# A delta-rule recurrence with a squared-ReLU feed-forward: the hand-written order of a program is replaced by a graph and a list builder

## The chip, the cores and the metric

The kernel runs on one NeuronCore of a Trainium2 chip. Its engines are TensorE (PE, with weight loads shown apart as PEld), VectorE (DVE), ScalarE (ACT), GpSimd (POOL) and SyncE (SP); each works through its own instructions in the order in which the program issues them. The metric is the time of one execution in microseconds (us) on the device.

## The reference

There are B=4 batches, H=8 heads, S=768 steps of time and D=40 columns. For each batch and head a 40 x 40 state is carried through time, and the outputs of all heads, put side by side (320 columns), go through a feed-forward layer of 2048 hidden columns:

```
state = 0
for t in range(768):
    y[t]  = r[t] @ state
    Sa    = state @ a[t]
    state = state * w[t] - outer(Sa, b[t]) + outer(v[t], k[t])
x = y with heads side by side                 # 3072 x 320
out = (max(x @ w_in, 0) ** 2) @ w_out         # 320 -> 2048 -> 320
```

## The kernel before

**Tiles and steps.** Time is cut into 6 chunks of 128 steps of time. Within a chunk the recurrence becomes matrix products between the 128 steps. A "batch" m (24 of them) is one chunk of one of the four batches of the data, with all 8 heads. A "step" st (48) is half of that, four heads, held as two pairs of heads. Eight steps make a chunk, and the state of a chunk goes to the next through the tile UZ.

**Preparing a batch.** Six loads (L81, queue of SP) bring w, k, b, a, v, r as NW to NR, with four buffers each; a small memset on POOL (L80) holds a later batch's loads back. prep_ln, prep_decay: logarithm of w, its running sum by a product (cs, L197), two exponentials GI and GA on ScalarE. POOL multiplies k and b by GI (KB, L206) and casts a, v, r (L183); prep_v copies v again from RV into EVX (L190). prep_kb, prep_ga, prep_rv turn these tiles on TensorE (tt, L214) and bring them out of PSUM as KBT, GT, AT and RVT.

**A step.** st_a_mm and st_a_ev: products ca (L260), masked into CN (VectorE, L268). st_p: products P. st_m: P is copied as Mc (ScalarE). st_corr, st_c1, st_corr, st_sn: two corrections of P by CN, with c1 on VectorE (L306) between them; ScalarE writes the result, negated, as Sn into EVX (L314). st_t: Sn and the carried state UZ are turned (tb, L339 and L345) and copied as TB (L350). st_ex_mm, st_ex_ev: products ex (L364), masked into EVX (L370). st_z, st_kb: products uy (L379, L389). st_y: uy becomes YS, the output of the step (L399), and UZ (L404).

**Half-array products.** ca and ex contract over 64 rows, and two of them stand in the upper and the lower half of the array; tb and uy write 64 columns each and stand side by side. The others use the whole array.

**Feed-forward.** It goes by "halves" h (12): four steps make one. gather copies a few rows within YS by four DMAs (L436) so that 8 heads of 40 rows lie in three groups. ffn_in makes a block of hidden columns (hp, L451; ReLU hs on ScalarE, L459; square Gt on POOL or VectorE, L461), eight a half. ffn_out sums over them (op, L478), two row blocks of two parts, copied out and stored (L482, L484).

**The order** is written by hand. The main loop runs over st and issues st_a_mm(st + 1), st_ex_mm(st - 1), st_p(st), st_y(st - 2) and so on; prepare(st, lot) issues a batch's preparation by a table, and filler(st) takes one hp or half an op from a queue that feed fills two steps after the gather. PSUM banks have fixed uses: two for ff (hp, op, cs, KB turned), ca0, ca1, ex0, ex1, sp (P, tb) and uy. warm(n) issues products without use, 54 in all.

Of the kernel before, what the change touches and what calls it, by code (L numbers as in the profile page):

```python
# [9 lines left out]
I32 = mybir.dt.int32  # L10
# [8 lines left out]
def kernel(  # L19
# [12 lines left out]

# [14 lines left out]
    AHEAD = 4  # L55
    HB = NB // 2
    NEV = 6

    gl = ctx.enter_context(tc.tile_pool(name="gl", bufs=1))
    chp = ctx.enter_context(tc.tile_pool(name="chp", bufs=2))  # L60
    qdp = ctx.enter_context(tc.tile_pool(name="qdp", bufs=3))
    ffp = ctx.enter_context(tc.tile_pool(name="ffp", bufs=3))
    ps = ctx.enter_context(tc.tile_pool(name="ps", bufs=1, space=PSUM))
    nat_cm = tc.tile_pool(name="natp", bufs=AHEAD)
# [7 lines left out]
    nat_srcs = {"W": w, "K": k, "V": v, "R": r, "A": a, "B": b}  # L72
    nat = {}

    def load(m, gate=True):
        c, bb = divmod(m, NB)
        for key in ("W", "K", "B", "A", "V", "R"):
            t_ = natp.tile([128, NHH, D], FP32, name=f"N{key}", tag=f"N{key}")
            if gate and key == "W":
                nc.gpsimd.memset(t_[0:1, 0, 0:1], 0.0)  # L80
            nc.sync.dma_start(  # L81
                out=t_[:],
                in_=nat_srcs[key][bb, :, c * L:(c + 1) * L, :].rearrange("h t e -> t h e"))
            nat[key, m] = t_

    for m in range(AHEAD):
        load(m, gate=False)
# [7 lines left out]
    ones_f = gl.tile([128, 128], FP32, name="ones_f")  # L95
    nc.gpsimd.memset(ones_f[:], 1.0)
    UTI = gl.tile([128, 128], FP32, name="UTI")
# [4 lines left out]
    ones_b = gl.tile([128, 128], BF16, name="ones_b")  # L102
    nc.vector.memset(ones_b[:], 1.0)
    nc.vector.memset(ACC[:], 0.0)
    IDb = gl.tile([128, 128], BF16, name="IDb")
# [4 lines left out]


    def warm(n):
        wu = ps.tile([128, 128], FP32, name="wu", tag="uy")
        for i in range(n):
            nc.tensor.matmul(out=wu[:], lhsT=ones_b[:], rhs=ones_b[:], start=True, stop=True)

    warm(26)
    MEX = gl.tile([128, 4, L], BF16, name="MEX")
# [6 lines left out]
    pads = {}  # L125
    for key, n in (("KB", 4), ("GA", 2), ("RV", 2)):
        pads[key] = []
        for i in range(n):
            t_ = gl.tile([128, len(key), NHH, 64], BF16, name=f"{key}p{i}")
            nc.vector.memset(t_[:, :, :, D:64], 0.0)  # L130
            pads[key].append(t_)
    MCN = gl.tile([128, 2, 2, L], BF16, name="MCN")
# [3 lines left out]
    GTs, RVs, EVXs, UZs, WIN = [], [], [], [], []  # L136
    for i in range(4):
        GTs.append(gl.tile([128, PB, L + 2], BF16, name=f"GT{i}"))
        nc.gpsimd.memset(GTs[i][:, :, 0:1], 1.0)
    for i in range(NEV):  # L140
        EVXs.append(gl.tile([128, 2, 2, EV], BF16, name=f"EVX{i}"))
        nc.gpsimd.memset(EVXs[i][:, :, :, 2 * LV:EV], 0.0)
    for i in range(4):
        t_ = gl.tile([128, 2, PB, LV], BF16, name=f"RV{i}")
        nc.gpsimd.memset(t_[:, :, :, L:LV], 0.0)
        for s in range(2):
            o_ = 64 * s
            nc.gpsimd.tensor_copy(  # L148
                out=t_[o_:o_ + D, 0, :, L:LV],
                in_=IDb[o_:o_ + D, o_:o_ + D].rearrange("p (u d) -> p u d", u=1)  # L150
                .to_broadcast([D, PB, D]))
        RVs.append(t_)
    for i in range(2):
        UZs.append(gl.tile([128, NP, 128], BF16, name=f"UZ{i}"))
    for g in range(PB - 1):
        WIN.append(gl.tile([128, DFF], BF16, name=f"WIN{g}"))
    for t_ in (UZs[1], WIN[2]):
        nc.vector.memset(t_[:], 0.0)
# [6 lines left out]
    bt = {}  # L165
# [4 lines left out]
    def prep_ln(m):  # L170
        o = bt[m] = Batch()
        o.RV, o.GA = (pads[key][m % 2] for key in ("RV", "GA"))
        o.KB = pads["KB"][m % 4]
        o.GT, o.RVT = GTs[m % 4], RVs[m % 4]
        o.EVX = [EVXs[(2 * m + u) % NEV] for u in range(2)]
        o.lnW = ffp.tile([128, NHH * D], FP32, name="lnW", tag="lnW", bufs=2)
        nc.scalar.activation(out=o.lnW[:], in_=nat.pop(("W", m))[:].rearrange("p h e -> p (h e)"),
                             func=ACTF.Ln)

    def prep_cast(m):  # L180
        o = bt[m]
        for key, pad in (("A", o.GA[:, 1]), ("V", o.RV[:, 1]), ("R", o.RV[:, 0])):
            nc.gpsimd.tensor_copy(out=pad[:, :, 0:D], in_=nat.pop((key, m))[:])  # L183
            if key == "V" and m == 0:
                prep_v(m)

    def prep_v(m):
        o = bt[m]
        for u in range(2):
            nc.gpsimd.tensor_copy(  # L190
                out=o.EVX[u][:, :, :, L:LV].rearrange("p i s e -> p (i s) e"),
                in_=o.RV[:, 1, 4 * u:4 * u + 4, 0:D])

    def prep_decay(m):
        o = bt[m]
        cs = ps.tile([128, NHH, D], FP32, name="cs", tag="ff", bufs=2)
        nc.tensor.matmul(out=cs[:].rearrange("p h e -> p (h e)"), lhsT=UTI[:], rhs=o.lnW[:],  # L197
                         start=True, stop=True)
        GI = ffp.tile([128, NHH, D], FP32, name="GI", tag="GI", bufs=2)
        nc.scalar.activation(out=GI[:], in_=cs[:], func=ACTF.Exp, scale=-1.0,  # L200
                             accum_out=ACC[:, AI + m:AI + m + 1])
        nc.scalar.activation(out=o.GA[:, 0, :, 0:D], in_=cs[:], func=ACTF.Exp,
                             accum_out=ACC[:, AG + m:AG + m + 1])
        for u, key in enumerate("KB"):
            eng = nc.vector if m < 2 and key == "B" else nc.gpsimd
            eng.tensor_tensor(out=o.KB[:, u, :, 0:D], in0=nat.pop((key, m))[:], in1=GI[:],  # L206
                              op=ALU.mult)

    def turned(pad, us=(0, 1), t_=None, **home):
        if t_ is None:  # L210
            t_ = ps.tile([128, 2, PB, L], BF16, name="tt", **home)
        for u in us:
            for j in range(PB):
                nc.tensor.transpose(  # L214
                    out=t_[:, u, j, :], identity=IDb[:],
                    in_=pad[:, u, 2 * j:2 * j + 2, :].rearrange("p a b -> p (a b)"))
        return t_

    def prep_rv(m):
        o = bt[m]  # L220
        t1 = turned(o.RV, tag="ex0")
        nc.vector.tensor_copy(out=o.RVT[:, :, :, 0:L], in_=t1[:])

    def prep_kb(m):
        o = bt[m]
        o.KBT = chp.tile([128, 2, PB, L], BF16, name="KBT", tag="KBT", bufs=3)
        t2 = turned(o.KB, tag="ff", bufs=2)
        nc.scalar.activation(out=o.KBT[:], in_=t2[:], func=ACTF.Copy)  # L228

    def prep_ga(m):  # L230
        o = bt[m]
        if m > 0:
            prep_v(m)
        o.AT = chp.tile([128, PB, L], BF16, name="AT", tag="AT", bufs=3)
        if m == 0:
            t3 = turned(o.GA, us=(0,), tag="ex0")
            nc.scalar.activation(out=o.GT[:, :, 1:L + 1], in_=t3[:, 0], func=ACTF.Copy)
            prep_kb(m)
            turned(o.GA, us=(1,), t_=t3)
        else:  # L240
            t3 = turned(o.GA, tag="ex0")
            nc.scalar.activation(out=o.GT[:, :, 1:L + 1], in_=t3[:, 0], func=ACTF.Copy)  # L242
        nc.vector.tensor_tensor(out=o.AT[:], in0=t3[:, 1], in1=o.GT[:, :, 0:L], op=ALU.mult)  # L243
# [3 lines left out]
    def where(st):  # L247
        c, q = divmod(st, NQ)
        return c, bt[c * NB + q // 2], (q % 2) * 2, slice(2 * q, 2 * q + 2), EVXs[st % NEV]

    CNs, Ps, SnTs, TBs, uys, Mc, Cc, YSs = {}, {}, {}, {}, {}, {}, {}, {}

    def st_a_mm(st):
        c, o, j0, p2, EVX = where(st)
        ca = CNs[st, "ps"] = [ps.tile([128, 2, 2, L], FP32, name=f"ca{s}", tag=f"ca{s}")
                              for s in range(2)]
        for u in range(2):
            for i in range(2):
                for s in range(2):
                    nc.tensor.matmul(out=ca[s][:, i, u, :], lhsT=o.KBT[half(s), u, j0 + i, :],  # L260
                                     rhs=o.AT[half(s), j0 + i, :], start=(i == 0 and u == 0),
                                     stop=True, skip_group_check=True)

    def st_a_ev(st):
        ca = CNs.pop((st, "ps"))
        CN = CNs[st] = qdp.tile([128, 2, 2, 2, L], BF16, name="CN", tag="CN")
        for s in range(2):
            nc.vector.tensor_tensor(out=CN[:, :, s], in0=ca[s][:], in1=MCN[:], op=ALU.mult)  # L268
# [54 lines left out]
    def st_energy(su):  # L323
        if su < 0 or su % (NQ // 2) > 1:
            return
# [398 lines left out]
```

## Time and profile before

| what | value |
|---|---|
| runs before | 323.8, 324.98, 325.31 us; median 324.98 |
| profiled execution, first to last instruction | 321.4 us; the record gives no time of its own around this span |
| granted TensorE clock, mean | 0.945 |
| busy: PE, PEld | 280.2 us (87%), 213.1 us (66%) |
| busy: DVE, POOL, ACT | 230.8 us (72%), 207.7 us (65%), 199.7 us (62%) |
| DMA | 31.37 MB, mean 98 GB/s |

The median of the runs is 3.6 us above the profiled span. Busy times are shares of the whole span; stages differ, so the times by stage say more. Products overlap on TensorE, so intervals between starts are read there, not durations.

### The profile page before, as it was taken

How to read it: one execution, taken by the hardware profiler on the slowest of the kernel's cores; microseconds unless marked ns; L12 is line 12 of the kernel's file. 1: busy time of each engine (PE TensorE's matmuls, PEld its weight loads, DVE VectorE, ACT ScalarE, POOL GpSimd, SP SyncE). 2: the span in 40 equal slices, each digit the busy share in tenths (PEclk: the TensorE clock that was granted, in tenths of full speed). 3: DMA queues.
4: the chain of work that ended last, by engine and by line, in shares of the span. 5: the costliest groups of instructions: out<-in, count | busy, mean ns of one | idle time of the engine just before them, and what ended most of it. 6: DMA issues, size and time to landing. Idle time of an engine off the chain costs nothing.

```text
span 321.4 us, 9886 instructions
## 1 busy us (share of the span) xinstructions
PE 280.2 (87%) x3880; PEld 213.1 (66%) x3880; DVE 230.8 (72%) x519; ACT 199.7 (62%) x529; POOL 207.7 (65%) x390
## 2 busy tenths in 40 slices
PE   6766758889999999999999999999999999979892
PEld 5544445576767767777776777777777677657581
DVE  6546777688887877888888788788888768663140
ACT  4344365378577676876866776695786767625461
POOL 8368467298678669667767866866876696534400
PEclk9778597599999999999999999999999999979999
DMA  7999999964475376457537636644762000000101
GB/s 130 174 167 174 185 160 170 161 107 87 85 143 98 78 126 111 89 99 125 105 71 144 111 70 115 118 94 87 133 111 52 26 6 22 27 3 21 34 35 51
DMA packets 158455, 31.37 MB, mean 98 GB/s; under 512 B 152944, under 2 KB 158080, under 8 KB 158400
## 3 DMA queue, kind: packets, MB, share of 16 engines
q1 hardware_dynamic: 155760, 28.02, 48.5%
q0 software_dynamic: 2640, 2.63, 5.2%
q8 instruction: 32, 0.52, 0.7%
q14 instruction: 23, 0.19, 0.2%
HBM read 28.84 MB, written 3.93 MB: 102 GB/s over the span
## 4 chain that ended last, share of the span: by engine, by line
PE 71%; ACT 13%; issue 7%; DVE 5%; POOL 2%; ACTq 0%; DVEq 0%; POOLq 0%
PE hp L451 16%; PE cs L197 6%; PE tt L214 5%; PE uy L389 5%; PE ca L260 5%; PE tb L339 4%; ACT hs L459 4%; PE ex L364 3%; ACT KBT L228 3%; PE P L298 3%; ACT EVX L314 2%; PE P L276 2%; ACT GT L242 2%; PE uy L379 2%; PE tb L345 1%
## 5 line engine op out<-in xcount | busy, mean ns | idle before, releaser
L451 PE MATMUL hp<-YS,WIN 120*128 120x256 bf16 (+1 forms) x576 | 78.0, 273 | 0.1
L461 POOL TENSOR_TENSOR Gt<-hs 128x512 bf16<-128x512 bf16 x66 | 67.8, 1042 | 13.5 <-ACT hs L459 12.5
L370 DVE TENSOR_TENSOR EVX<-ex,MEX 128x512 bf16<-128x512 f32 x96 | 65.8, 686 | 4.7 <-PE ex L364 3.0
L459 ACT ACTIVATE hs<-hp 128x512 bf16<-128x512 f32 x96 | 57.6, 600 | 16.1 <-PE hp L451 14.4
L268 DVE TENSOR_TENSOR CN<-ca,MCN 128x512 bf16<-128x512 f32 x96 | 61.4, 681 | 0.8 <-PE ca L260 0.8
L451 PEld LDWEIGHTS <-WIN 120*128 120x128 bf16 (+1 forms) x576 | 49.8, 97 | 6.5 <-issue 0.5
L206 POOL TENSOR_TENSOR KBp<-NK,GI 128x320 bf16<-128x320 f32 x24 | 21.1, 880 | 38.5 <-ACT GI L200 37.1
L478 PEld LDWEIGHTS <-Gt 128*128 128x128 bf16 x384 | 35.0, 98 | 12.8 <-issue 0.2
L318 POOL TENSOR_TENSOR Cc<-x,EVX 128x160 bf16<-128x160 f32 x48 | 23.4, 487 | 25.9 <-ACT EVX L314 23.7
L317 POOL TENSOR_TENSOR x<-Mc,c 128x160 f32<-128x160 bf16 x48 | 23.3, 485 | 15.3 <-DVE c L306 14.3
L306 DVE TENSOR_TENSOR c<-P,Mc 128x160 bf16<-128x160 f32 x48 | 15.6, 325 | 23.6 <-POOL RVp L183 10.7
L320 ACT ACTIVATE jk<-CN 128x512 bf16<-128x512 bf16 x48 | 30.6, 637 | 0.0
L339 PE MATMUL tb<-IDb,EVX 128*64 128x128 bf16 x192 | 15.0, 238 | 15.7 <-ACT EVX L314 15.7
L298 PEld LDWEIGHTS <-CN 128*128 128x128 bf16 x384 | 21.0, 97 | 10.4 <-issue 9.8
L350 DVE COPY TB<-tb 128x512 bf16<-128x512 bf16 (+1 forms) x48 | 19.1, 397 | 11.2 <-PE tb L345 8.3
L228 ACT ACTIVATE KBT<-tt 128x1024 bf16<-128x1024 bf16 x24 | 24.5, 1019 | 4.1 <-PE tt L214 4.1
L291 ACT ACTIVATE Mc<-P 128x160 bf16<-128x160 f32 x48 | 14.8, 307 | 18.2 <-PE P L282 18.2
L399 DVE TENSOR_TENSOR YS<-uy,GT 128x256 bf16<-128x256 f32 x48 | 20.1, 418 | 7.0 <-PE uy L389 6.7
L339 PEld LDWEIGHTS <-EVX 128*64 128x64 bf16 x192 | 6.9, 110 | 26.9 <-ACT EVX L314 26.5
L243 DVE TENSOR_TENSOR AT<-tt,GT 128x512 bf16<-128x512 bf16 x24 | 10.2, 425 | 19.5 <-ACT GT L242 16.5
L389 PE MATMUL uy<-EVX,KBp 128*64 128x168 bf16 x384 | 23.8, 249 | 0.0
L197 PE MATMUL cs<-lnW,UTI 128*128 128x320 f32 x48 | 22.0, 544 | 0.3 <-POOL RV L148 0.3
(132 smaller groups left out, 609.9 us busy)
## 6 DMA issues: line engine op xcount, KB each, us to landing
NW<-in_w_dram SPq DMA_DIRECT2D x24, 160.0 KB, 2.8
NK<-in_k_dram SPq DMA_DIRECT2D x24, 160.0 KB, 3.7
NB<-in_b_dram SPq DMA_DIRECT2D x24, 160.0 KB, 3.6
NA<-in_a_dram SPq DMA_DIRECT2D x24, 160.0 KB, 3.9
NV<-in_v_dram SPq DMA_DIRECT2D x24, 160.0 KB, 4.6
NR<-in_r_dram SPq DMA_DIRECT2D x24, 160.0 KB, 3.6
out_dram<-osb SPq DMA_DIRECT2D x24, 160.0 KB, 1.8
WOUT<-in_moe_w_out_dram POOLq DMA_DIRECT2D x1, 1280.0 KB, 11.2
```

The source lines that it names most:

```text
L197: nc.tensor.matmul(out=cs[:].rearrange("p h e -> p (h e)"), lhsT=UTI[:], rhs=o.lnW[:], start=True, stop=True)
L228: nc.scalar.activation(out=o.KBT[:], in_=t2[:], func=ACTF.Copy)
L268: nc.vector.tensor_tensor(out=CN[:, :, s], in0=ca[s][:], in1=MCN[:], op=ALU.mult)
L298: nc.tensor.matmul(out=P[:, i, s, 0:D], lhsT=CN[:, i, s, 1, :], rhs=X[:, 2 * i + s], start=False, stop=last, skip_group_check=True)
L320: nc.scalar.activation(out=jk[:], in_=CN[:, :, :, 1, :], func=ACTF.Square, accum_out=ACC[:, AN + st:AN + st + 1])
L339: nc.tensor.transpose(out=tb[half(s), i, :], in_=EVX[:, i, s, L + LV:EV], identity=IDb[:])
L370: nc.vector.tensor_tensor(out=EVX[:, :, s, 0:2 * LV].rearrange("p i (u x) -> p i u x", u=2)[:, :, :, 0:L], in0=exs[st][s][:], in1=MEX[:].r ...
L389: nc.tensor.matmul(out=uy[half(s), i, :], lhsT=o.KB[:, u, 2 * (j0 + i) + s, :], rhs=EVX[:, i, s, LV * u:LV * u + LV], start=(c == 0 and i ...
L451: nc.tensor.matmul(out=hp[:, u, :].rearrange("p (a b) -> p a b", a=HB), lhsT=WIN[g][0:ROWS[g], j * 128:(j + 1) * 128], rhs=by_pair(c, hf)[ ...
L459: nc.scalar.activation(out=hs[:], in_=flat, func=ACTF.Relu)
L461: later.append(lambda: eng.tensor_tensor(out=out_, in0=hs[:], in1=hs[:], op=ALU.mult))
L478: nc.tensor.matmul(out=op_[:], lhsT=Gts[c, hf][:, j, b_, :], rhs=WOUT[:, j, :], start=(j == 0), stop=(j == NJ - 1))
```

## The change

The program is the same computation. Each operation now is an entry of a graph: name, engine, rank, cost, latency, what it needs, which buffers it uses. A function listed() goes through them with a clock of its own and puts them into one order; then they are issued in that order. Buffers belong to rings with a number of places each (RING); the eight PSUM banks are common to all uses, with at most four for hp and op and three for a batch's preparation. From step 12 on ca(st) and ex(st - 3) are one entry R, and uy's products of step st - 4 and tb of step st - 2 are one entry C. The V cast goes from NV into EVX directly. EVX, KB and GT have five buffers by batch. The first batch is prepared in two halves. The warm-up products after the first 26 are gone, and so are POOL's small memsets ahead of the loads.

```diff
-    def prep_v(m):
-        o = bt[m]
-        for u in range(2):
-            nc.gpsimd.tensor_copy(
-                out=o.EVX[u][:, :, :, L:LV].rearrange("p i s e -> p (i s) e"),
-                in_=o.RV[:, 1, 4 * u:4 * u + 4, 0:D])
+            if key == "X":
+                nc.gpsimd.tensor_copy(
+                    out=o.EVX.tile[:, j0:j0 + n, :, L:LV].rearrange("p i s e -> p (i s) e"),
+                    in_=o.nat["V"].tile[:, h])
...
+    NBANK = 8
+    CAP = {"ff": 4, "prep": 3}
+    RING = {"N": 4, "lnW": 2, "GI": 2, "KB": 5, "GA": 2, "RV": 2, "EVX": 5, "RVT": 4, "KBT": 3,
+            "AT": 3, "GT": 5, "CN": 3, "c1": 3, "x1": 3, "jk": 1, "jm": 1, "Mc": 2, "Cc": 2,
+            "TB": 9, "UZ": 2, "YS": 3, "hs": 3, "Gt": 2, "osb": 3}
...
+        op(("L", m, key), "DQ", rank, 0.97, 3.0, [], [o.nat[key]], go)
...
+        def go():
+            nc.gpsimd.dma_start(out=WOUT[:], in_=moe_w_out.rearrange("(j p) f -> p j f", p=128))
+        op(("WOUTq",), "DQ", -1.5, 8.3, 8.3, [], [], lambda: None)
+        op(("WOUT",), "POOL", -1.5, 0.5, 1.0, [("WOUTq",)], [], go)
...
+            def gather(p=p, row=row, hh=hh, e0=e0, n=n):
+                src = 64 * (hh % 2) + e0
+                nc.sync.dma_start(out=by_pair()[row:row + n, p], in_=by_pair()[src:src + n, hh // 2])
+            op(("mv", h, x), "SP", st0 + 7.3 + 0.01 * x, 0.1, 2.0, done, [X_], gather)
...
+            rank = st0 + 8.0 + 0.45 * jj
+            op(("hp", h, jj), "PE", rank, *pe(0.654),
+               [("mv", h, x) for x in range(len(MOVED))] + [("WIN", g) for g in range(NG)],
+               [X_, hpb], ff_in, "F")
...
+    for st in range(MERGE, NS):
+        merge(("R", st), [("ca", st), ("ex", st - 3)], st, "R")
+        merge(("C", st), [("kbm", st - 4), ("tb", st - 2)], st + 0.01, "C")
...
+    SWITCH, SLACK = 0.095, 0.06
+    BIAS = {"FR": 0.3, "FC": 0.6, "CR": 0.3}
+    START = {"PE": 4.0, "ACT": 2.2, "DVE": 4.0, "POOL": 5.2, "SP": 0.9, "DQ": 0.9}
...
+                t0 = min(t for t, _ in cand) + SLACK
+                t, o = min(((t, o) for t, o in cand if t <= t0),
+                           key=lambda x: (x[1].rank + BIAS.get(mode + (x[1].mode or mode), 0.0),
+                                          x[1].order))
...
+    plan = listed()
...
+    for t, o in plan:
...
+        o.fn()
```

In the new names kbm is the product into uy by KB, z the carried one, mv a copy of the gather, hs and Gt the ReLU and the square, and DQ a queue that exists in the list alone: the loads are issued by SP, in the list's order among SP's own entries.

More of the change, by code (lines that the diff above doesn't have):

```diff
@@ new lines, with buf, op @@
+    class Op:
+        __slots__ = ("name", "eng", "rank", "cost", "lat", "needs", "bufs", "mode", "fn", "end",
+                     "order")
+    ops, rings = {}, {}
+    def buf(ring, kind=None):
+        b_ = Buf(ring, kind)
+        if ring != "bank":
+            row = rings.setdefault(ring, [])
+            b_.n = len(row)
+            row.append(b_)
+        return b_
+    def op(name, eng, rank, cost, lat, needs, bufs, fn, mode=None):
+        o = Op()
+        o.name, o.eng, o.rank, o.cost, o.lat, o.mode = name, eng, rank, cost, lat, mode
+        o.needs, o.bufs, o.fn, o.end, o.order = list(needs), list(bufs), fn, None, len(ops)
+        for b_ in o.bufs:
+            b_.users.append(o)
+        assert name not in ops, name
+        ops[name] = o
@@ new lines, in merge @@
+    def merge(name, parts, rank, mode):
+        olds = [ops.pop(p) for p in parts]
+        bufs = []
+        for o in olds:
+            for b_ in o.bufs:
+                b_.users.remove(o)
+                if b_ not in bufs:
+                    bufs.append(b_)
+        def go():
+            for o in olds:
+                o.fn()
+        cost = sum(o.cost for o in olds)
+        op(name, "PE", rank, *pe(cost), [n for o in olds for n in o.needs], bufs, go, mode)
+        for p in parts:
+            alias[p] = name
@@ L109 @@
     )
[L112 to L118, printed above, removed]
+    for i in range(26):
+        nc.tensor.matmul(out=banks[NBANK - 1][:, 0:128], lhsT=ones_b[:], rhs=ones_b[:], start=True,
+                         stop=True)
     nc.vector.memset(MEX[:], 1.0)
@@ L153 @@
-    for i in range(2):
[L154 to L158, printed above, removed]
+    for i in range(2):
+        for ring in ("GT", "EVX", "RVT"):
+            blank(ring, i)
+    later = {}
+    for ring, a_, b_, eng, cost in (("KB", 2, 5, "DVE", 0.21), ("UZ", 1, 2, "DVE", 1.0),
+                                    ("GT", 2, 5, "POOL", 0.05), ("EVX", 2, 5, "POOL", 0.2),
+                                    ("RVT", 2, 4, "POOL", 1.1), ("UZ", 0, 1, "DVE", 1.0)):
+        for i in range(a_, b_):
+            rank = i - 1.5 if ring != "UZ" else (7.0, 0.5)[i]
+            later[ring, i] = ("blank", ring, i)
+            op(("blank", ring, i), eng, rank, cost, cost + 0.05, [], [],
+               lambda ring=ring, i=i: blank(ring, i))
@@ L160, in half, with cleared @@
+    def cleared(ring, i):
+        i %= RING[ring]
+        return [later[ring, i]] if (ring, i) in later else []
     def half(s):
         return slice(64 * s, 64 * s + 64)
-    bt = {}
+    nat_srcs = {"W": w, "K": k, "V": v, "R": r, "A": a, "B": b}
+    SPLIT = 1
     class Batch:
         pass
[L170 to L178, printed above, removed]
@@ L209, in turned @@
[L209 to L222, printed above, removed]
@@ L224, in prep_kb @@
[L224 to L243, printed above, removed]
@@ L247, in where @@
-    def where(st):
-        c, q = divmod(st, NQ)
[L249 to L257, printed above, removed]
+    bt = []
+    for m in range(NBC):
+        o = Batch()
+        bt.append(o)
+        o.nat = {key: buf(f"N{key}") for key in "WKBAVR"}
+        o.lnW, o.GI, o.KB, o.GA, o.RV, o.EVX, o.RVT, o.KBT, o.AT, o.GT = (
+            buf(x) for x in ("lnW", "GI", "KB", "GA", "RV", "EVX", "RVT", "KBT", "AT", "GT"))
+        for x in ("KB", "GA", "RV", "EVX", "RVT", "GT"):
+            getattr(o, x).tile = fixed[x][m % RING[x]]
+        o.parts = [(0, 2), (2, 2)] if m < SPLIT else [(0, PB)]
@@ new lines, in tb_ev, with ex_mm @@
+        def tb_ev():
+            hi = 4 if carry else 2
+            nc.vector.tensor_copy(out=sb(TB_, [128, 4, 128], BF16)[:, 0:hi], in_=tbv()[:, 0:hi])
+        def ex_mm():
+            R, V = o.RVT.tile[:, 0], o.RVT.tile[:, 1]
+            for u in range(2):
+                for i in range(2):
+                    for s in range(2):
+                        lhsT = TB_.tile[half(s), i, :] if u else V[half(s), j0 + i, 0:L]
+                        nc.tensor.matmul(out=quads(ex[s])[:, i, u, :], lhsT=lhsT,
+                                         rhs=R[half(s), j0 + i, 0:L], start=(i == 0 and u == 0),
+                                         stop=True, skip_group_check=True)
@@ new lines, in add_step @@
+        op(("ex", st), "PE", st + 3.0, *pe(0.225), [("TB", st), ("RVT", m, p)],
+           [TB_, o.RVT] + ex, ex_mm, "R")
+        for s in range(2):
+            op(("EVX", st, s), "DVE", st + 3.05 + 0.02 * s, 0.6, 0.685, [("ex", st)],
+               [ex[s], o.EVX], lambda s=s: ex_ev(s))
+        op(("kbm", st), "PE", st + 4.01, *pe(0.285),
+           [("EVX", st, 0), ("EVX", st, 1), ("Sn", st)] + [("kb", m, key, p) for key in "KB"],
+           [o.KB, o.EVX, uyb], kb_mm, "C")
+        last = ("kbm", st)
```

880 lines of the change are left out of this document (509 added, 371 removed).

## The prediction

> **What bounds the kernel now.** I read the page's slices first, then busy time and clock by stage, then TensorE's timeline over one steady pair of steps, then SyncE's issues.
>
> ```profile
> PE   6766758889999999999999999999999999979892
> PEclk9778597599999999999999999999999999979999
> DMA  7999999964475376457537636644762000000101
> ...
> 24.00:37.00 13.00, 8.61 (x118) 5.94 (x116) 9.43 (x22) 5.25 (x15) 9.57 (x21) 0.76 1.02 176
> 50.00:62.00 12.00, 9.20 (x108) 6.35 (x108) 7.20 (x18) 5.74 (x16) 6.51 (x15) 0.64 1.08 159
> 84.00:152.00 68.00, 63.85 (x969) 49.84 (x969) 55.48 (x127) 48.15 (x131) 50.41 (x90) 1.00 0.59 105
> ```
>
> The last three lines are stages: length, then busy time of PE, PEld, DVE, ACT and POOL, granted clock, DMA share, GB/s. Up to 62 us there are no feed-forward products to fill TensorE: eight steps take 52 us at a clock of 0.64 to 0.76. After that TensorE is the bound: 63.85 of 68 us.
>
> ```profile
> 157.40 0.82 PE L451 MATMUL hp<-YS,WIN 120*128 120x256 bf16 x6
> 158.91 0.30 PE L339 MATMUL tb<-IDb,EVX 128*64 128x128 bf16 x4 [0.69 <-ACT EVX L314]
> 159.04 0.28 PE L345 MATMUL tb<-IDb,UZ 128*64 128x128 bf16 x4
> 159.16 0.46 PE L389 MATMUL uy<-EVX,KBp 128*64 128x168 bf16 x8
> 159.55 0.40 PE L260 MATMUL ca<-AT,KBT 64*128 64x128 bf16 x8
> ```
>
> Starts are what counts, as products overlap. A pair of steps (one batch) lasts 11.4 us (hp at 151.85 and again at 163.25), and one wait stands in it: the second step's transposes (st_t) come 0.69 us late, because ScalarE's Sn (L314) ends the correction chain late. All else is work. One hp is 0.66 us (155.74 to 156.40) and half an op is 1.08 (161.62 to 162.70). A change between full-array and half-array products costs about 0.09: hp to tb 0.75 instead of 0.66.
>
> **Time base.** The profiled span is 321.4 us and the median of the runs 324.98 (323.8 to 325.31), so 3.6 us lie around the span. I sum against 321.4 and add 3.6. Half a per cent, 1.6 us, is about what a measurement of this kernel can tell from no change.
>
> **Grouping and banks.** The merged R (ca with ex of three steps before) and C (uy with tb of two steps before) should save changes of array mode. Counted in the order of products, the old program has 215 changes and the new one 205; in the steady part a pair goes from 8 to 7. From 62 us on that is 18 x 0.09 = 1.6 us gained, no more. Common banks: idle time before hp is 0.1 us in all now, so there is nothing to gain; a bank that comes late costs one eviction (0.6 to 0.69 us), for which I put nothing: the list waits for banks by its own figures (0.60 for CN and EVX), and these agree with the spacing of the rows.
>
> **V into EVX.** 48 copies of 318 ns (13.9 us of POOL) become casts from NV, 453 ns by the row of RVp<-NV, 24 of them: 10.9 us. The 20 gate memsets (1.8 us) go too. POOL is busy 50.4 of 68 us beside TensorE, so this is worth nothing on the path; without that cover it would be worth 4.8.
>
> **Waits taken out.** tb now stands two steps behind its Sn, so the waits at L339 should go: 18 x 0.69 plus one of 0.39 from 62 us on, 12.8 us. The end has further losses: ex on TB 0.58 and 0.54, P on c 0.51, ep on jm 1.40 and 1.7 us by a stretch at half clock (below). Together 17.5 us gained. What is next late in their place is the gather.
>
> **The gather, where the new list is short.** In the old order a half's four copies YS to YS are issued two steps before its first hp. The new list puts hp of half h as soon as its figures allow: SP cost 0.1 us a copy and 2.0 us to land, 2.3 in all. The trace has:
>
> ```profile
> 95.23 3.82 SPq L436 DMA_DIRECT2D YS<-YS  x4
> 118.10 3.08 SPq L436 DMA_DIRECT2D YS<-YS  x4
> ...
> DMA to landing us min/median/max: 1.7/1.8/6.2
> ```
>
> An issue holds SP's queue for 0.77 us, so the fourth lands at 3 x 0.77 + 1.8 = 4.1 us, or 5.0 where the list puts a load (0.89) among them. Before it come UZ and YS on VectorE (0.48 + 0.34 + latency, 1.0 us; up to 2.4 where evictions stand ahead). TensorE's list holds between the last z of a half and its hp: h=2 4.8 us, h=3 5.9, h=4, 6, 8 4.0, h=5, 7 3.7, h=9, 10 3.6. Against 5.2 to 6.6 us of gather that leaves waits of 0.75 to 2.4 us, 14 over nine halves. All that follows on TensorE stands behind this wait in order: C, R, the corrections. I take 13, as an issue can take 0.62 (bounds 8 and 20, the second by the longest issues). At the tail only two op halves (2.17 us) cover 5.5 us: 3.3 more, where the old tail covers it with 4.4 us of op.
>
> **The start.** POOL's clears, the halved first batch and the removed order should bring ca(0) from 10.5 to about 9 us and the first eight steps from 58 to about 48, since VectorE needs 34 us for them (CN and EVX 32 x 0.60, c 8 x 0.33, TB, YS, UZ 8 x 1.0, RVT and AT 4 x 1.0) and cannot be kept full. Two things push it back. POOL now issues weights among kb and casts (rows: 2.26, 2.08 and 1.06 us, where the list counts 0.3), which puts kb of batch 3 at about 28 us; WIN(2) follows it and lands 5.3 us after issue, so hp(0,0) starts at about 37.6, some 3 us late. And the list holds WOUT back until its own figures have the transfer done:
>
> ```profile
> WOUT<-in_moe_w_out_dram POOLq DMA_DIRECT2D x1, 1280.0 KB, 11.2
> ```
>
> Its issue stands behind the square of hp(0,2), at about 43 us, so it lands at 54, while TensorE reaches op(0,0) after 5 to 7 us of work, at about 48. Behind op(0,0) stand cs(4) and kbm(7), so YS(7) comes at about 58 and hp(1,0) at 62 (56 to 66). By then TensorE has done, beyond what the old program has at 62, seven hp (4.6), two op halves (2.2), two uy and an ex (1.1): 8 us gained (2 to 14). Of it go 2 us where tGA(5) waits for loads that SP holds behind the second gather, and 1.5 in steps 14 to 16, which have no hp to fill them.
>
> **Sum.** 321.4 - 1.6 - 17.5 - 8 + 13 + 3.3 + 2 + 1.5 = 314.1; with 3.6 around it 317.7, so 318.
>
> **A rule against it: the clock.** Waits of 2 us are what cools TensorE:
>
> ```profile
> 283.00:286.00 3.00, 1.73 (x32) 1.11 (x32) 2.95 (x7) 1.26 (x5) 1.97 (x3) 0.96 0.00 0
> 286.00:288.00 2.00, 2.00 (x10) 1.16 (x9) 0.34 (x1) 0.23 (x1) 0.00 (x0) 0.50 0.04 8
> ```
>
> After 3 us in which TensorE was busy 1.73 us, the clock is at half for some 3.4 us, a loss of 1.7. One wait of 0.69 us per pair never did this from 84 to 266 us. The Trainium skill (TensorE: Matmul & The Clock Gate, Part 1, HAM oscillation) asks for idle gaps above about 3.4 us before the clock falls; by it the gather's waits cost nothing beyond themselves and the sum stays 318. The trace disagrees: before 285.8 us no single gap was above 0.6 us, and the clock fell all the same, so I let the row decide and keep the case as a rival.
>
> **Rivals.**
> - *The gather is hidden.* If other small waits already put TensorE behind its list, the copies land in time, and WOUT may land in 8 us, free of loads: 318 - 13 - 3.3 - 2 = about 300. For it: ScalarE, VectorE and POOL all have 20% and more idle to keep up. Against: those waits would have to be as long as the gather's.
> - *The clock cools, slower than before.* If each of nine gather waits costs a window of 1.7 us, and two windows more in the start, it is 318 + 18.7 = 336. It decides from the sixth cooled window on (318 + 6 x 1.7 = 328). For: the row above, 28 of the 54 warm-up products are gone, and the old start already has some 31 us at half clock (twice the missing share of the clock column). Against: a wait of 1.2 us with dense hp around it looks more like the 0.69 us that did no harm.
> - *VectorE's order makes corrections late, slower than before.* In the new list c1 stands behind RVT, a square, EVX and CN (0.60 + 0.34 + 0.60 + 0.60 = 2.1 us), and the second correction comes 2.85 us after P on TensorE; P, Mc and the first correction use the rest. VectorE is 82% busy in 84 to 152. Over 40 steps 0.3 us each is 12 us: 330. It decides above 0.22 us a step. Against: half the steps stand behind a gather wait, in which VectorE catches up.
>
> **How the numbers follow.** The sum has 0.45 (its own range 311 to 325, by the bounds of gather and start), four fifths of it faster: 0.36 faster, 0.09 the same. Hidden gather 0.21, faster. Clock 0.18: 0.02 the same, 0.16 slower. VectorE 0.16: 0.01 the same, 0.15 slower. So faster 0.57, same 0.12, slower 0.31. For 8 in 10 the range goes down to the hidden gather, 300, and up to most of the two slow cases, 333.
>
> **What would show it.** Right: no wait of tb on ScalarE; idle time before the first hp of each half, ended by the YS copies, 1 to 2.5 us each; one wait of 4 to 8 us of op on WOUT near 50 us; hp from about 38 us; about 3.3 us idle before the last half's hp. Wrong: hp never waits (then 300 or less); the granted clock falls between 70 and 270 us; or c1 and the corrections carry the waits. The forecast fails most simply if hp(1,0) does not come within 56 to 66 us.

## The result, and the profile after

The changed kernel takes 337.54 us (median; 336.73 to 339.54) against 324.39 us (323.29 to 325.31) for the kernel before, measured beside it: a ratio of 1.042, 95% interval 1.038 to 1.047. It is slower. The forecast was 318, its range 300 to 333. The profiled span is 335.6 us at a mean granted clock of 0.92 (before: 321.4 us at 0.945).

First the slices of the page, in the rows that were shown of before:

```profile
PE   6798675578999599899699699899899898998894
PEclk9559959599999879999899979999999999799978
DMA  8996296439999698699725744633000001001011
```

Two things are new. Between slices 10 and 30, where the old PE row held 9 throughout, every third slice or so stands at 5, 6 or 8. And the clock row, which was 9 there, dips in three places. What TensorE waited for (engine, operation, releaser: us in total, times, longest), first the largest entry of before, then the changed kernel:

```profile
PE tb L339 <- ACT EVX L314: 15.7, 24, 1.1
```

```profile
PE bank L630 <- DMA YS<-YS: 24.1, 19, 2.8
PE bank L658 <- DMA WOUT<-in_moe_w_out_dram: 7.1, 1, 7.1
PE bank L294 <- POOL KB L279: 2.1, 4, 1.4
PE bank L498 <- DVE EVX L487: 1.5, 3, 1.0
```

L630 is hp, L658 op. The 15.7 us of tb behind ScalarE's Sn are gone, as forecast. In their place stand 24.1 us behind the gather and 7.1 us behind WOUT. Waits of the corrections on c (0.5 us) and Mc (1.4 us) are small. The stages show the price (length; busy PE, PEld, DVE, ACT, POOL; granted clock, DMA share, GB/s):

```profile
50.00:62.00 12.00, 5.18 (x76) 3.67 (x74) 6.35 (x15) 3.99 (x9) 6.43 (x8) 0.92 0.80 112
84.00:152.00 68.00, 61.87 (x911) 48.54 (x911) 53.74 (x123) 48.17 (x130) 51.73 (x86) 0.95 0.94 161
```

In the same 68 us from 84 us on, the old kernel did 969 products at a clock of 1.00; the new one does 911 at 0.95. And from 50 to 62 us TensorE is busy for 5.2 of 12 us: that is the wait for WOUT. The timelines of TensorE and of SyncE's queue at half 2 and at WOUT:

```profile
62.27 2.29 PE L658 MATMUL bank<-WOUT,Gt 128*128 128x320 bf16 x8 [7.10 <-DMA WOUT<-in_moe_w_out_dram]
...
72.61 0.73 PE L630 MATMUL bank<-YS,WIN 120*128 120x256 bf16 x5 [1.23 <-DMA YS<-YS]
...
114.84 0.39 PE L630 MATMUL bank<-YS,WIN 120*128 120x256 bf16 x1 [2.60 <-DMA YS<-YS]
116.36 3.81 PE L630 MATMUL bank<-YS,WIN 120*128 120x256 bf16 x17 [1.13 <-DMA YS<-YS]
```

```profile
110.49 0.61 SPq L244 DMA_DIRECT2D NV<-in_v_dram  x1
111.19 4.00 SPq L620 DMA_DIRECT2D YS<-YS  x4
```

A half's first hp comes in two pieces: one product starts when the first copies are there, the other five wait for the last one. In half 2, VectorE began to write YS at 109.2 us, but SyncE first issued loads that stood ahead in its queue, then took 4.0 us for the four copies; hp went on at 116.36, 7.2 us after the start of YS. In halves 7, 9, 10 and 11, which have no loads ahead of the copies or among them, the same chain takes 4.7 us.

### The profile page after: what moved, and what is told of

The parts are those of the page before. It is cut to its first block, busy times and chain, and to the rows that moved or that the text cites. A ratio compares the mean times of both kernels' runs of the same rounds, so it can differ in the third digit from the quotient of the medians.

```text
span 335.6 us, 9943 instructions
## 1 busy us (share of the span) xinstructions
PE 286.5 (85%) x3852; PEld 221.8 (66%) x3852; DVE 228.9 (68%) x523; ACT 203.7 (61%) x531; POOL 205.0 (61%) x350
## 4 chain that ended last, share of the span: by engine, by line
PE 51%; DMA 15%; DVE 14%; SPq 7%; POOL 4%; issue 4%; ACT 4%; DVEq 0%; POOLq 0%; ACTq 0%
PE bank L630 18%; PE bank L658 10%; DMA YS<-YS 7%; SPq L620 6%; PE bank L294 6%; DVE EVX L487 4%; PE bank L498 4%; DVE CN L402 3%; DMA WOUT<-in_moe_w_out_dram 3%; PE bank L263 3%; PE bank L394 2%; DMA NW<-in_w_dram 2%; PE bank L426 2%; DMA NA<-in_a_dram 2%; POOL KB L279 2%
## 5 line engine op out<-in xcount | busy, mean ns | idle before, releaser
L630 PE MATMUL bank<-YS,WIN 120*128 120x256 bf16 (+1 forms) x576 | 86.4, 294 | 24.7 <-DMA YS<-YS 24.1
L636 ACT ACTIVATE hs<-bank 128x512 bf16<-128x512 f32 x96 | 57.0, 598 | 50.7 <-PE bank L630 44.8
L630 PEld LDWEIGHTS <-WIN 120*128 120x128 bf16 (+1 forms) x576 | 56.1, 104 | 43.4 <-DMA YS<-YS 24.7
L487 DVE TENSOR_TENSOR EVX<-bank,MEX 128x512 bf16<-128x512 f32 x96 | 65.1, 684 | 14.0 <-PE bank L482 12.8
L402 DVE TENSOR_TENSOR CN<-bank,MCN 128x512 bf16<-128x512 f32 x96 | 64.6, 682 | 4.2 <-PE bank L394 3.7
L658 PE MATMUL bank<-WOUT,Gt 128*128 128x320 bf16 x384 | 60.1, 302 | 7.1 <-DMA WOUT<-in_moe_w_out_dram 7.1
L658 PEld LDWEIGHTS <-Gt 128*128 128x128 bf16 x384 | 35.6, 98 | 20.1 <-issue 7.1
L279 POOL TENSOR_TENSOR KB<-NK,GI 128x320 bf16<-128x320 f32 (+1 forms) x25 | 21.2, 850 | 24.1 <-ACT GI L268 23.8
L342 ACT ACTIVATE KBT<-bank 128x1024 bf16<-128x1024 bf16 (+1 forms) x25 | 24.7, 987 | 9.7 <-PE bank L294 7.8
L498 PE MATMUL bank<-EVX,KB 128*64 128x168 bf16 x384 | 24.7, 248 | 1.7 <-DVE EVX L487 1.5
L263 PE MATMUL bank<-lnW,UTI 128*128 128x320 f32 x48 | 21.0, 523 | 1.2 <-ACT lnW L257 0.9
L511 DVE TENSOR_TENSOR YS<-bank,GT 128x256 bf16<-128x256 f32 x48 | 20.2, 421 | 2.5 <-PE bank L505 2.1
## 6 DMA issues: line engine op xcount, KB each, us to landing
WOUT<-in_moe_w_out_dram POOLq DMA_DIRECT2D x1, 1280.0 KB, 10.2
```

Source lines behind the costliest of these rows:

```text
L263: nc.tensor.matmul(out=csb.tile[:, 0:NHH * D], lhsT=UTI[:], rhs=o.lnW.tile[:], start=True, stop=True)
L279: eng.tensor_tensor(out=o.KB.tile[:, u, h, 0:D], in0=o.nat[key].tile[:, h], in1=o.GI.tile[:, h], op=ALU.mult)
L342: nc.scalar.activation(out=t_[:, :, j0:j0 + n], func=ACTF.Copy, in_=bank(b2)[:, 0:2 * n * L].rearrange("p (u j t) -> p u j t", u=2, t=L))
L402: nc.vector.tensor_tensor(out=t_[:, :, s], in0=quads(ca[s]), in1=MCN[:], op=ALU.mult)
L487: nc.vector.tensor_tensor(out=EVX[:, :, s, 0:2 * LV].rearrange("p i (u x) -> p i u x", u=2)[:, :, :, 0:L], in0=quads(ex[s]), op=ALU.mult, ...
L498: nc.tensor.matmul(out=uy()[half(s), i, :], lhsT=o.KB.tile[:, u, 2 * (j0 + i) + s, :], rhs=EVX[:, i, s, LV * u:LV * u + LV], start=(i == 0 ...
```

## The experiments

The theory after the first reading: three losses make the difference, (1) the waits for the gather, since the list holds a copy for 0.1 us of SyncE and puts too little work ahead of hp; (2) stretches at half clock that these waits cause; (3) the late WOUT. The rivals: VectorE and the corrections are the real limit, so that other waits come when these go; and the half clock costs nothing or has another cause. Ratios are to runs of the kernel before on the same chip.

**The gather left out** (same order, copies not issued).

```diff
-                nc.sync.dma_start(out=by_pair()[row:row + n, p], in_=by_pair()[src:src + n, hh // 2])
+                pass
```

> The order of the changed kernel with the 48 copies of the gather left out (the rows that they move are not moved; hp is computed on what stands there). It prices the gather with all that hangs on it. Theory A (sum of waits 24.1 us, and half clock in the middle caused by them, 13.6 us long and so up to 6.8): 337.5 - 24 - 5 = about 308, and no stretch at half clock between 75 and 280 us. Rival B (other engines are late too): 320 to 330, with TensorE waiting on c, CN or EVX instead. Rival C (half clock comes from something else than the waits): about 313, and the stretches at half clock stay.

Measured: 303.42 us, ratio 0.934 (0.928 to 0.941), less than the 308 expected. The profile of this run in the two steady stages:

```profile
84.00:152.00 68.00, 65.74 (x1015) 52.85 (x1014) 59.18 (x136) 52.01 (x143) 54.34 (x91) 1.00 0.99 176
152.00:220.00 68.00, 67.71 (x1046) 56.40 (x1045) 59.86 (x135) 53.81 (x142) 54.50 (x86) 1.00 0.48 92
```

The record of the granted clock has no stretch at half speed from 65.8 to 301 us. So the gather with all that hangs on it costs 34.1 us, and the rest of the new order is good: without it TensorE is busy 67.7 of 68 us, and from 62 us on no wait for a correction reaches 0.6 us. The rival of VectorE falls, here and in the prediction. It is also where the prediction's rival of a hidden gather (about 300) lies.

**The list told what a copy costs** (0.8 us in place of 0.1; then 1.0 us, with 3.0 us to land).

```diff
-            op(("mv", h, x), "SP", st0 + 7.3 + 0.01 * x, 0.1, 2.0, done, [X_], gather)
+            op(("mv", h, x), "SP", st0 + 7.3 + 0.01 * x, 0.8, 2.0, done, [X_], gather)
```

> The list is told 0.8 us for each copy of the gather instead of 0.1; nothing else is changed. It then puts about 5.4 us of work by its own figures on TensorE between the end of a half and its first hp, where it put 3.6. Theory A (waits for the gather are missing work in the order): the wait of hp falls from 24.1 us to below 10, the stretches at half clock between 110 and 200 us go with it (another 4 to 6 us), and the time falls by 12 to 20 us, to 318 to 326. Rival B (VectorE and the corrections are the real limit, and the gather's wait only hides it): the time falls by less than 5 us and waits of TensorE on VectorE or ScalarE come in its place.

> The changed kernel with only the list's figures for a copy of the gather changed, to 1.0 us and 3.0 us for the landing; weights late as they were. With 0.8 and 2.0 it gave 321.35, with 1.0 and 3.0 and early weights 308.96. Theory A (weights and gather add up): 308.96 + 8.7 = 316 to 319. Rival B (with more work ahead of hp, TensorE reaches op(0,0) later, so the late WOUT is covered and early weights bring nothing): 309 to 312.

Measured: 321.35 us, ratio 0.990 (0.986 to 0.994), waits for copies 8.2 us; with 1.0 and 3.0, 316.10 us, ratio 0.972 (0.969 to 0.975), waits 7.3 us. The second lies where it should if this and earlier weights (below) add up. The clock did not come as expected: with 0.8 and 2.0 it still fell at 112.3 us (6.8 us long) and 139.6 us (3.4 us), behind waits of 3.1 us on Mc and of 2.0 us on the copies. One number in a table, and the change is no longer slower. Work for TensorE was there; the list had no reason to put it ahead of hp.

**Two queues for the copies, the order unchanged.** This tells apart too little work ahead of hp from four issues in a row on one queue.

```diff
-            def gather(p=p, row=row, hh=hh, e0=e0, n=n):
+            def gather(x=x, p=p, row=row, hh=hh, e0=e0, n=n):
...
-                nc.sync.dma_start(out=by_pair()[row:row + n, p], in_=by_pair()[src:src + n, hh // 2])
+                (nc.scalar if x % 2 else nc.sync).dma_start(out=by_pair()[row:row + n, p], in_=by_pair()[src:src + n, hh // 2])
```

> The order of the changed kernel, with two of each four copies issued by ScalarE instead of SyncE. Theory A (the wait is the four issues in a row on SyncE's queue, 0.6 to 0.9 us each, with loads between them in halves 2 to 6): the last copy is issued some 1.7 us sooner, 2.5 to 3 us in halves 2 to 6, so that the wait of hp falls from 24.1 us to 4 to 10 us, half clock in the middle goes, and the time falls to 310 to 320. Rival B (ScalarE now waits in order for YS ahead of Mc, hs and Sn, and 24 issues of about 0.7 us stand in its queue): waits of TensorE on ScalarE come in the place of the gather's, 328 to 338.

Measured: 316.58 us, ratio 0.979 (0.970 to 0.987), waits for copies 5.8 us. One stretch at half clock is left in the middle, 110.4 to 117.2 us, around a wait of 2.0 us for copies. What an issue holds of a queue, first in the changed kernel, then in this one (min/median/max in ns):

```profile
L620 SPq DMA_DIRECT2D YS<-YS x48: 620/820/1743, 37.4 to 317.9; - x48
```

```profile
L620 SPq DMA_DIRECT2D YS<-YS x24: 779/821/1862, 36.4 to 295.9; - x24
L620 ACTq DMA_DIRECT2D YS<-YS x24: 592/606/1437, 36.4 to 295.7; - x24
```

An issue on ScalarE's queue takes 0.6 us, and ScalarE starts no activation in that time:

```profile
106.51 0.61 ACTq L620 DMA_DIRECT2D YS<-YS  x1
106.78 0.18 ACT L451 ACTIVATION_READ_ACCUMULATOR jk<-CN 128x1 f32 x1
107.16 0.61 ACTq L620 DMA_DIRECT2D YS<-YS  x1
107.82 0.30 ACT L529 ACTIVATE Mc<-bank 128x160 bf16<-128x160 f32 x1 [0.86 <-PE bank L294]
```

In none of the 24 issues did one start. What was begun before runs on, and Mc starts 0.05 us behind the second issue. Two issues of 1.3 and 1.4 us were paid for by TensorE, with a wait of 1.3 us on Sn and one of 1.4 us on Mc right behind them; the waits on Mc grew from 1.4 to 4.3 us in all. So the two queues trade a long wait for short ones. Both readings hold: the wait can be taken away by work ahead of hp, or by a shorter row of issues. Here half of the copies also no longer stand behind SyncE's loads, and this run does not tell the two apart. The Trainium skill (DMA: Bandwidth & Descriptors, Anatomy of one DMA) counts, for a DMA that GpSimd issues, some 50 ns of dispatch and a small, variable part for descriptors within a fixed cost of about 2 us; if that held on SyncE's queue too, four copies would land almost together, as the list assumes. The trace differs: 0.82 us for each issue.

**TensorE kept busy in the waits.** Products without use before the first hp of halves 2 to 9, 69 in all where the expectation counts 74, as many as fit the wait; all else unchanged.

```diff
+                if jj == 0:
+                    for _ in range({2: 16, 3: 6, 4: 14, 5: 11, 6: 5, 7: 5, 8: 7, 9: 5}.get(h, 0)):
+                        nc.tensor.matmul(out=hpb.tile[:], lhsT=ones_b[:], start=True, stop=True,
+                                         rhs=MEX[:].rearrange("p i x -> p (i x)"))
```

> The changed kernel with products without use put on TensorE ahead of the first hp of halves 2 to 9, as many as fit into the wait that its profile shows there (74 of 128 x 512, 0.21 us each at full clock, 15.8 us in all of 17.7 us of waits in these halves). The waits stay, but TensorE is not idle in them. Theory A (idle time in the waits cools the clock, and the half clock costs up to 6.8 us between 110 and 200 us): no stretch at half clock from 75 to 280 us, and 337.5 falls by 3 to 7 us, to about 332. Rival B (half clock costs nothing, since other work is late there, or it is not caused by the waits): the time stays at 336 to 339 or grows.

Measured: 328.38 us, ratio 1.015 (1.008 to 1.021), 9.2 us less than the changed kernel, more than expected. The wait at half 2, first in the changed kernel, then here:

```profile
114.00:121.00 7.00, 5.03 (x38) 3.57 (x40) 1.08 (x3) 2.33 (x6) 3.33 (x6) 0.55 0.77 125
```

```profile
112.00:119.00 7.00, 6.69 (x83) 4.79 (x82) 3.15 (x8) 4.12 (x10) 4.31 (x9) 1.00 0.87 139
```

In the changed kernel the clock falls at 114.7 us, as the first wait of half 2 (2.6 us) ends, and stays at half for 6.8 us; at 165.9, 193.2 and 285.3 us stand 3.4 us each. Here there is none from 65 to 311 us. Five such units of 3.4 us, up to 1.7 us lost in each, make at most 8.5 us. Of the 8.6 us between the two profiled spans, 1.7 stand already at 97 us, ahead of the first product without use; 6.9 are left. So the half clock is caused by idle time in the waits, and it is paid.

**Weights earlier.** First WOUT alone is issued where the list begins its transfer; then all weights, and the memset of WIN's third group, for which GpSimd had waited 2.5 us, ahead of the first group.

```diff
-        op(("WOUTq",), "DQ", -1.5, 8.3, 8.3, [], [], lambda: None)
-        op(("WOUT",), "POOL", -1.5, 0.5, 1.0, [("WOUTq",)], [], go)
+        op(("WOUTq",), "DQ", -1.5, 8.3, 8.3, [], [], go)
+        op(("WOUT",), "POOL", -1.5, 0.5, 1.0, [("WOUTq",)], [], lambda: None)
```

> The order on all engines stays as in the changed kernel; only the issue of WOUT moves forward on GpSimd, to the place where the list begins its transfer (behind the V cast of batch 3, at about 36 us instead of 52). Theory A (WOUT is late by its issue, and all later work hangs behind that wait): it lands near 48 us, the wait of op(0,0) of 7.1 us goes, hp(1,0) comes at 63 to 66 us instead of 71, the time falls by 6 to 8 us from 337.5, to about 330. Rival B (the first 60 us are bound by the loads and VectorE, so TensorE would wait there anyway): the wait turns into others, hp(1,0) stays above 69 us and the time within 2 us of 337.5. Rival C (only the clock counts): it depends on whether a stretch at half clock near 60 us goes, 3 us at most.

> The order of the changed kernel, with all weights (WIN and WOUT) issued where the list begins their transfers, and the memset of WIN's third group ahead of the first group. Moving WOUT alone gave 331.0 and left hp a wait of 4.1 us for WIN's third group, which stood behind WOUT. Theory A: neither hp nor op waits for weights now, hp(0,0) starts before 40 us, hp(1,0) at 58 to 64, and the time is 325 to 329. Rival B (the loads of batches 3 and 4 are pushed back by the weights): waits for KB and GA take the place, and the time stays at 330 or above.

Measured: WOUT alone 331.0 us (one run at 324.75, three at 330.4 to 331.8, so no ratio is given); all weights 328.84 us, ratio 1.013 (1.008 to 1.017), 8.7 us less than the changed kernel. With WOUT alone the wait moved (profile of the run at 331.77):

```profile
PE bank L630 <- DMA YS<-YS: 25.5, 20, 4.0
PE bank L630 <- DMA WIN<-in_moe_w_in_dram: 4.1, 1, 4.1
```

With WOUT alone hp(1,0) began at 66.7 us, not 63 to 66. With all weights early, no wait for weights is left, and hp(1,0) begins at 65.0 us instead of 71.1, five of its six products at 66.5 instead of 72.6. It was expected by 64. hp(0,0), expected before 40, came at 46.2, after a wait of 4.2 us for its own gather: later than in the changed kernel (41.1).

**Early weights and fill together**, to see whether they add up.

> All weights early (328.8 alone) and products without use in the waits of halves 2 to 9 (328.4 alone), with the order of the changed kernel and all its waits for the gather. Theory A (start and clock are separate losses, and they are what the sum of the prediction missed): 337.5 - 8.7 - 9.2 = 319.6, within 2 us, so near the forecast of 318, and what is left above it is the gather's wait, 24 us instead of some 18. Rival B (both come from the same half clock): 325 to 328.

Measured: 325.30 us, ratio 1.002 (0.999 to 1.005). They do not add up: 3.5 us below early weights alone. The timelines show part of it. In half 3 YS came at 123.9 us, but SyncE issued the first copy at 126.0, as loads stood ahead; in the run without fill YS came at 126.3 and the first copy at 126.8. In half 6 it is 1.3 us against 0.5. So 2.5 us of what a warm TensorE gains are waited for again behind the loads. The rest of the difference, some 3 us, stays open.

**Weights early and the list's 1.0 and 3.0 us**, then the same without grouping R and C.

> Weights as in the run with all weights early, and the list is told 1.0 us for each copy of the gather and 3.0 us for its landing, so that it puts 6.5 to 7 us of work by its own figures between a half's end and its first hp. With 0.8 and 2.0 (5.4 us of work) it gave 321.35 with 8.2 us of waits for the gather and 4.6 for WOUT left. Theory A (only missing work in the order): waits for gather below 3 us, none for weights, 310 to 315. Rival B (the order pays elsewhere: corrections and preparations come late since hp no longer fills in): 318 to 325.

> The same version (308.96) with R and C not grouped; the list has 7.8 us of work there instead of 6.7 between a half and its first hp, so the gather is hidden in both. Forecast of the prediction: grouping is worth 1.6 us, so 309 to 312. Rival B (grouping keeps the order apart from the gather's needs, as its removal gained 6.4 us in the changed kernel): 305 or below. Rival C (more switches of array mode cost more than 0.09 us each): 313 or above.

Measured: 308.96 us, ratio 0.951 (0.946 to 0.956), waits for copies still 10.0 us, not below 3; without grouping 317.14 us, ratio 0.976 (0.973 to 0.979). In the changed kernel itself taking the grouping out had the other sign:

```diff
-    SU, MERGE = 4, 12
+    SU, MERGE = 4, 48
```

> The changed kernel with R and C not grouped (ca, ex, kbm and tb as entries of their own through all steps). Forecast of the prediction: grouping is worth 1.6 us. Theory A: the time is 1 to 4 us above 337.5, unless the order that comes out leaves more work between a half and its hp: here the list has 4.8 us there instead of 3.6, which by the account of the gather is worth 8 x 1.1 = 9 us, so that the time falls to about 330. Rival B (grouping matters and the gather does not): slower than 338.5.

Measured: 331.10 us, 6.4 us below the changed kernel, ratio 1.022 (1.012 to 1.031). The waits for copies are 19.9 us here instead of 24.1, and 13.6 in place of 10.0 in the pair above, and from 67 us to the last few us three units at half clock stand in place of six, and five in place of three. With 1.7 us a unit and 1.9 us for grouping itself (below) that makes −7.4 and +8.9 us, against −7.9 and +10.2 between the profiled executions. Why the waits rose in the second pair stays open: by the list's own figures the order without grouping has more work ahead of hp in both (4.8 against 3.6 us, 7.8 against 6.7). To price grouping alone, the gather was left out:

> Ungrouped R and C in the order of the list, with the 48 copies of the gather left out (their rows are not moved). It prices the grouping where no gather can wait; with grouping the same kernel took 303.42. Theory A (grouping is worth its changes of array mode and no more, 1.6 us by the prediction): 304 to 307. Rival B (grouping is worth the 8.2 us by which 317.14 lies above 308.96 in the versions with the gather): 310 to 313, with no waits on copies and no half clock between 70 and 280 us. Rival C (grouping costs time, since without it the changed kernel gained 6.4 us): below 302.

Measured: 305.36 us, 1.9 us above the 303.42 with grouping; no half clock from 66 to 302 us. The difference is the size of the forecast's 1.6, though the two were run in separate comparisons and their ratios' intervals (0.935 to 0.949, 0.928 to 0.941) overlap.

**The V cast alone**, put into the kernel before.

```diff
-            nc.gpsimd.tensor_copy(out=pad[:, :, 0:D], in_=nat.pop((key, m))[:])
+            nc.gpsimd.tensor_copy(out=pad[:, :, 0:D], in_=(nat[key, m] if key == "V" else nat.pop((key, m)))[:])
...
-                in_=o.RV[:, 1, 4 * u:4 * u + 4, 0:D])
+                in_=nat["V", m][:, 4 * u:4 * u + 4])
```

> The kernel before, with one part of the change alone: the V part of EVX is cast from NV and not copied from RV. Forecast of the prediction: nothing on the path, 324 within 1 us. Rival: GpSimd's copies matter at the start or where NV is held longer and holds loads back, up to 3 us slower.

Measured: 324.12 us, ratio 0.999 (0.996 to 1.002). Nothing, as forecast.

**The end, and a version that beats both kernels.** To early weights and the dearer gather, later ranks for half 10 are added (hp + 2.0, op + 3.0), so that the last gather is covered; then the two queues.

> The version with early weights and the dearer gather in the list (308.96), with hp of half 10 ranked 2.0 later and its op 3.0 later, so that kbm(47), z(47) and the gather of the last half come ahead of them and 6.3 us of work by the list's figures cover the last gather, where 2.2 did. Its profile has two waits there of 1.68 and 1.92 us, and 6.8 us at half clock from 289.7 us. Theory A: the waits go, and with them the stretch at half clock: 3.6 + 3.4, so 302 to 304. Rival B (ep or the copies out of the last products set the end): 306 or more.

> The fastest version so far (306.11) with two of each four copies issued by ScalarE. It has 6.0 us of waits for copies left, 2.1 of them before hp of half 2, with loads between the copies. Theory A: these go, 302 to 305. Rival B (ScalarE's wait for YS delays Mc and hs): 307 to 312.

Measured: 306.11 us, ratio 0.944 (0.940 to 0.949), and 300.79 us, ratio 0.925 (0.916 to 0.934). With the later ranks the waits of the last half and its half clock are gone, but 2.9 us were gained by the medians, not 5 to 7. The two profiled executions lie 5.0 us apart, and the runs of this version spread over 3.4 us, so the size is not settled. Its profile has a new stretch of 3.4 us at half clock at 105.8 us, behind a wait of 2.1 us for copies in half 2, which the two queues then took away. The slices of the last version, and the one wait for copies that it has left:

```profile
PE   6797887998999988999999999999999999999992
PEclk9555665999999999999999999999999999999999
```

```profile
PE bank L630 <- DMA YS<-YS: 1.8, 1, 1.8
```

From 52.8 us to the last microsecond there is no half clock. The same graph, with the weights issued earlier, the copy's cost put right, two ranks changed and a second queue, takes 7.5% less time than the kernel before.

## Why the prediction was wrong, step by step

The mechanism that it took for the likeliest was there: waits of tb gone, waits of hp on the copies in their place. The sum missed by 19.8 us (317.7 against 337.5), in three terms.

- **The clock was taken as a rival, and it belonged in the sum.** This is the step that failed in kind. The prediction argued that "a wait of 1.2 us with dense hp around it looks more like the 0.69 us that did no harm". But its own sum had waits of up to 2.4 us. At the waits of halves 2, 4 and 5, which add up to 3.7, 3.3 and 2.6 us within each half, the clock fell every time; after waits of 1.1 to 1.7 us in halves 3, 6, 7 and 8 it did not, and near half 9 (1.2 us) it did. Price: at most 8.5 us by five units, 6.9 by the profile with fill, once its earlier start is taken off. That the prediction listed "the granted clock falls between 70 and 270 us" as what would make it wrong was the right test. The Trainium skill (TensorE: Matmul & The Clock Gate, Part 1, HAM oscillation) has the clock fall at idle gaps over some 3.4 us; ahead of the stretch at 165.9 us the longest single wait was 1.9 us, so the trace disagrees again. The Trainium skill also has, in the section A second HAM failure mode of the same page, many short idle times that make the clock fall and rise; that is nearer to what is seen here.
- **The start was mis-sized.** hp(0,0) was to come at 37.6 us and came at 41.1, five of its six products at 44.2; hp(1,0) was to come at 62 us (56 to 66) and came at 71.1, five of its six at 72.6. WOUT was to be issued at 43 us and was at 52.0, and the wait was 7.1 us, within the 4 to 8 forecast, but 8 us later. What the forecast left out: GpSimd stood 2.5 us behind VectorE's memset of WIN's third group and 6.4 us behind a c that hp(0,0) held up on TensorE, and hp(0,0) itself waited 2.8 us for a gather that the sum counted only from half 2 on. So hp(1,0) was 10.6 us late, and the 8 us that were to be gained here became a loss of 2.6. Early weights won 8.7 us back.
- **The gather was a little dearer.** Halves 2 to 10 waited 17.4 us, where 13 was taken and 8 to 20 bounded; the last half 2.4, where 3.3 was put. The issue was sized right: four copies hold SyncE's queue for 3.07 us in most halves, where 3.08 was taken. Short were the loads ahead of the first copy, which in halves 2 and 4 starts 2.0 and 1.0 us behind YS, against 0.45 in halves without; that is 2.1 of the 4.4 us by which halves 2 to 10 are over, and the rest is not taken apart. With the 0.9 us by which the last half is under, 3.5 us in all.

These are 6.9 to 8.5, 10.6 and 3.5 us. The terms of 2 us (tGA(5)) and 1.5 us (steps 14 to 16) came at most in part: the largest wait of that kind is 0.8 us. Without them the three make 17.5 to 19.1 of the 19.8 us. One more unit at half clock, up to 1.7 us at 319.5 us in the last half, is in neither sum, so the account closes to within some 2 us, no better.

Right were the size of the 1.6 us for grouping (1.9 measured, too small a difference to be clear of noise), nothing for the banks and the V cast, nothing for VectorE and the corrections, and the waits of tb taken out. The rival at 336 us gave nearly the measured time for a partly wrong reason: six units of half clock between 84 us and the last 3 us, not nine, no more half clock in the start than before (30.7 us in both profiles, not two units more), and a late start for the rest.

## What to carry to other kernels

A list builder is as good as its figures for the resources that look free: a small DMA's issue holds its queue, and four of them in a row ahead of a dense product are a wait for which the list must have work at hand. When a forecast contains idle time on TensorE in pieces of some 2 us, put the half clock behind them into the sum, not beside it; most such pieces brought it here, though not all (a wait of 2.3 us in the run at 308.96 did not). And price a part of a change where nothing else can wait: taking the grouping out measured −6, +8 and +2 us, and only the last, with the gather left out, comes near its own cost.

## What the hardware showed that was not expected

- The clock changes on a grid of 3.41 us, and the idle share of TensorE in one such stretch goes with a fall. In the profiles of all runs, from 62 us to 3 us before the end, 34 stretches at full clock ended in a fall; their idle share, from the rows of the products, was 0.41 to 0.92. Those that ended without one had up to 0.51. So below 0.41 the clock never fell here, and above 0.51 it always did. In the changed kernel TensorE was busy 0.77 of the 3.41 us before the fall at 165.9 us, 1.93 before that at 285.3, and 2.04 in the stretch from 258.0 to 261.4 us, after which the clock stayed. So not only a wait's length counts, but also where it lies on the grid and what idle time stands beside it.
- Half clock in the start was not free. The changed kernel and the run with fill have the same products in the same order up to 110 us. Up to 67 us the first has 3.4 us more at half clock in its record, and at 97 us it is 1.7 us behind.
- The clock row reads 9 also where the record has no entry. In the run with early weights and the dearer gather the record begins at 30.3 us; up to then the products of L294 start 107 ns apart, from 36 to 42 us 56 ns, so TensorE ran at half speed there, and the mean clock of 0.97 for this run is too high.
- A DMA issue on ScalarE's queue took 0.61 us and let no new activation start in the run with the order unchanged; 24 of them brought TensorE waits on Mc of up to 1.4 us.
